# Output weights of an attention kernel: block operations one per slot, second half in the last pair step, left(0) ahead of the last value sums

## The chip, the core and the metric

The kernel runs on one core of one Trainium2 chip. The metric is the device time of one execution in microseconds (us). The core has five engines with instruction streams of their own: PE (matrix products; its weight loads are listed as PEld), DVE, ACT and POOL (elementwise work), and SP, which here issues nearly all DMA transfers, in one order fixed at build time. An engine takes its instructions strictly in order and waits on semaphores for what other engines or transfers have to finish first.

## The reference

Two independent computations on inputs of 2048 rows by 576 columns; their results stand side by side in an output of 2048 x 1152, all float32. Cut to what matters:

```python
# A: attention with a compressive memory, 32 heads of 18 columns, 4 segments of 512 rows
for s in range(4):
    logits = q_s @ k_s.T * 18 ** -0.5 + mask          # mask: -1e9 where the key index is above the query's
    a_dot = softmax(logits) @ v_s
    pq = phi(q_s)                                     # phi(t) = t + 1 if t > 0 else exp(t)
    a_mem = (pq @ M) / (pq @ z + 1e-6)
    o_s = g * a_mem + (1 - g) * a_dot                 # g = sigmoid(beta), one per head
    pk = phi(k_s); M += pk.T @ v_s; z += pk.sum(0)
A = concat(o_s) @ wo                                  # 2048 x 576 by 576 x 576
# B: Fourier mixing, real part of a two-dimensional DFT given as matrices
a = x @ hid_re.T; b = x @ hid_im.T
B = seq_re @ a - seq_im @ b                           # 2048 x 2048 by 2048 x 576, twice
return concat([A, B], axis=-1)
```

The change lies in how the operands of the product `o @ wo` are prepared.

## The kernel before

**Products.** A float32 product is done as three products of rounded parts: an operand is split into a high part (a copy in the rounded type, made on ACT) and a low part (operand minus high part, made on DVE or POOL), and high x low, high x high and low x high are added up in PSUM.

**Stages.** First come the projections and the memory. Then two streams of work are interleaved to the end. `dense()` does the Fourier mixing: `hidden` makes a and b, `sequence` multiplies by the DFT matrices through `product` (PE lines L583 and L628 to L630), whose operand blocks `chi`/`clo` are split as they arrive (L451 on ACT, L456 on POOL), and its result is evacuated into `y` on DVE (L653). `attention()` does the heads. It is a generator over 68 steps p of eight slots each; 64 steps belong to pairs of heads, and the stages of one pair are spread over steps by lags (scores first, softmax parts 2 and 3 steps later, the value products `pv` 4 steps later), so steps 64 to 67 only drain. The main loop runs one slot of `attention()`, then pieces of `dense()` until both streams have used the same share of their estimated time; so an engine's queue holds slots of attention and pieces of dense work in turn. `later(n, ...)` runs a thing n slots later.

**The last steps of attention.** `pv(n)` (L1066, L1067 on PE) multiplies probabilities by values into the one PSUM bank `pv`; `pv_out` (L1079 to L1088 on DVE, "value sums" below) normalises what is there, reads the bank empty and adds the share to `og`. The probabilities' low parts are made by L1049 on DVE. Six slots after the second half of a group of four heads, `turn_out` transposes `og` (L1101, DVE) and its store to `od` follows; after the last group `turn_tails` (L1113) transposes the tails, stores them to `odt`, and one more transfer copies `odt` into `od`.

**The output stage.** `o @ wo` is done by 2 x 2 blocks with seven products instead of eight (p1 to p7), for row tiles n and n + 8 together, n = 0 to 7, in two column halves of `wo`'s inner blocks (c = 0 and 1). It needs combined operands on both sides:

- Right operands, from `wo` in five row blocks `raw[0]` to `raw[4]` (the last is a 64-row tail, held twice). For a half c the blocks are a = c and b = c + 2. `first_block` gives B11, `second_row` B21 and B22, `tails` and `tail_difference` the tail operands. Four subtractions (`difference`, L739) form, in place in `raw`, aR - aL, bR - aR, bR - aL and bL - bR (L and R are the left and right 288 columns); `combined` makes their high parts on ACT (L707) and `combined_low` their low parts on DVE (L710). `block_low` and `row_low` make low parts on POOL (also L710).
- Left operands: `left(n)` (L805 to L846), from the rows that come back from `od`: sums and differences of two row tiles and their splits. For n = 0 its two-operand instructions are on DVE (L825, L828, L829, L832, L833, L837, L840, L843, L845) and its copies on ACT (L826, L830 and others). It is a generator of six pieces.

`o_load` (L687) loads a row tile back from `od`; `o_pair` does that for n and n + 8 into `craw`. In `output_stage`, p7 and p6 and the others issue their products through `seventh` (L848, matmul L857), p7 ends with two `u` sums on DVE (among them L879), and `store` writes rows of the output.

**What sets the order.** All right operands are prepared while attention and the dense work are still running. `right_operands` fills a table `PLAN` at build time: `at(p, slot, fn, ...)` runs `fn` right behind the issue of that slot of step p. So an operation's place in its engine's queue, and that of a DMA in SP's queue, is what the table says. `ready` in the main loop is the generator `left(0)`, which is started at step 67 slot 5 and then takes one piece a slot or piece of dense work.

Of the kernel before, what the change touches and what calls it, by code (L numbers as in the profile page):

```python
# [12 lines left out]
F32 = mybir.dt.float32  # L13
# [9 lines left out]
S, D, H, DH, NSEG, L = 2048, 576, 32, 18, 4, 512  # L23
P = 128
# [16 lines left out]
def infini_attention_and_fnet(ctx: ExitStack, tc: tile.TileContext, xT, wqk, w8, wv, wo, beta, xtT, cT, hT, out):  # L41
    nc = tc.nc
    act, dve, pool, pe = nc.scalar, nc.vector, nc.gpsimd, nc.tensor
# [100 lines left out]
    def wide_tile(cols):  # L144
        return lambda: wide.tile([P, cols], F32R, name="wide", tag="wide")
# [196 lines left out]
    def sums(c):  # L342
        b, at, both = SUMS[c]
        if c < 4:
            return m_ps[b][:, at:at + 1 + both]
        return m_ps[b][:64, at].rearrange("p (k h) e -> p k h e", k=2)
# [349 lines left out]
    def right_operands():  # L696
        raw, late = {}, {}

        def at(p, slot, fn, *a):
            PLAN.setdefault(8 * p + slot, []).append((fn, a))  # L700

        def load(k):
            raw[k] = sb.tile([P, D], F32, name="raw", tag="raw", bufs=3)
            dma(raw[k], wo[k])

        def high(o, k, cs=slice(0, D)):
            act.activation(o, raw[k][:, cs], AF.Copy)  # L707

        def low(engine, o, hi, k, cs=slice(0, D), rows=slice(0, P)):
            engine.tensor_tensor(o[rows], raw[k][rows, cs], hi.bitcast(F32)[rows], OP.subtract)  # L710
# [30 lines left out]
        def stage(i, n):  # L741
            return (sr if i < 2 else sq).tile([P, 4, 256], F32R, name="late", tag=f"{n}s{i}").rearrange("p a x -> p (a x)")

        def combined(c, n):
            k, names = ((c, ("T1", "T3")), (c + 2, ("T4", "T2")))[n]
            if c == 0:
                hi, lo = late["s", n] = [stage(n, x) for x in "qk"]
                lo = [lo[:, L_], lo[:, R_]]
            elif n == 0:
                hi, lo = [stage(2, x) for x in "qk"]  # L750
                lo = [lo[:, L_], lo[:, R_]]
            else:
                hi, lo = wide_tile(D)(), [t[:, D:D + 288] for t in late["s", 0]]
            for i, x in enumerate(names):
                WO[x, c] = hi[:, 288 * i:288 * i + 288], lo[i]
            high(hi[:, :D], k)

        def combined_low(c, n):
            k, names = ((c, ("T1", "T3")), (c + 2, ("T4", "T2")))[n]
            for i, x in enumerate(names):  # L760
                low(dve, WO[x, c][1], WO[x, c][0], k, (L_, R_)[i])

        def block_low(c):
            low(pool, WO["B11", c][1], WO["B11", c][0], c, L_)
# [1 line left out]
        def row_low(c):  # L766
            low(pool, late["r", c][1], late["r", c][0], c + 2)

        at(57, 2, load, 0)
        at(57, 4, load, 2)  # L770
        at(58, 2, first_block, 0)
        at(58, 2, second_row, 0)
        at(58, 2, load, 4)
        at(58, 4, block_low, 0)
        at(59, 4, row_low, 0)
        at(59, 2, tails)
        at(60, 4, lambda: low(pool, late["w"][0], late["w"][0], 4, rows=lower))
        at(61, 4, lambda: low(pool, late["w"][1], late["w"][1], 4, rows=upper))
        at(61, 6, difference, pool, (4, L_), (4, L_), (4, R_))
        at(62, 2, tail_difference)  # L780
        at(62, 4, lambda: low(pool, TAIL[0][0], TAIL[0][0], 4, L_, lower))
        at(62, 6, lambda: low(pool, TAIL[0][1], TAIL[0][1], 4, L_, upper))
        at(62, 6, load, 1)
        at(63, 6, first_block, 1)
        at(64, 4, block_low, 1)
        for c, p in ((0, 64), (1, 66)):
            a, b = c, c + 2
            if c:
                at(65, 6, load, 3)
                at(66, 2, second_row, 1)  # L790
                at(66, 3, row_low, 1)
            at(p, 3 + c, difference, dve, (a, L_), (a, R_), (a, L_))
            at(p, 3 + c, difference, dve, (a, R_), (b, R_), (a, R_))
            at(p, 5 + c, difference, dve, (b, R_), (b, R_), (a, L_))
            at(p, 5 + c, difference, dve, (b, L_), (b, L_), (b, R_))
            for n in range(2):
                at(p + 1, 2, combined, c, n)
                at(p + 1, 3 + n, combined_low, c, n)
        for t in (0, 8):
            at(66, 5, o_load, t, lambda t=t: sq.tile([P, 4, 256], F32, name="oraw", tag="qs3" if t else "ks3").rearrange(  # L800
                "p a x -> p (a x)")[:, :5 * P].rearrange("p (k x) -> p k x", k=5))
        for t, tag in ((1, "phi"), (9, "plo")):
            at(67, 4, o_load, t, lambda tag=tag: sa.tile([P, 5, P], F32, name="oraw", tag=tag, bufs=2))

    def left(n):  # L805
        one, two = O.pop(n), O.pop(n + 8)
# [389 lines left out]
        tick()  # L1196
    td = ta = 0.0
    right_operands()
    ready = None
    for n, w in enumerate(attention()):  # L1200
        tick()
        ta += w
        for fn, a in PLAN.pop(n, ()):
            fn(*a)
        if n == 8 * (NP + V_LAG - 1) + 5:
            ready = left(0)
        if ready:
            next(ready, None)
        while td / total_d < ta / total_a:
            t = next(d, BREAK)  # L1210
            if t is BREAK:
                break
            td += t
    while due:
        tick()
    for t in d:
        tick()
        next(ready, None)
    while due:
        tick()  # L1220
    for _ in ready:
        pass
    output_stage()


# [41 lines left out]
```

## Time and profile before

| | |
|---|---|
| device time, median of 3 runs | 999.08 us (998.12 to 999.17) |
| the profiled execution: time, span, mean granted TensorE clock | 998.66 us, 997.0 us, 0.998 |
| PE busy | 982.3 us, 99% of the span, 9246 instructions |
| PE weight loads busy | 919.6 us, 92% |
| DVE busy | 787.3 us, 79%, 2115 instructions |
| ACT busy | 714.6 us, 72%, 1686 instructions |
| POOL busy | 673.8 us, 68%, 744 instructions |
| DMA | 209.97 MB, mean 211 GB/s |

The time is that of the whole execution on the device; the span is from the first to the last instruction in the trace of one profiled execution. Busy times are sums over that span. A group row names line, engine, operation, result <- operands with their shapes, then count, busy time and the idle time of the engine in front of it with what ended it. In a window row the first number pair is the window in us from the start of the span. Durations in the trace belong to that one execution.

### The profile page before, as it was taken

Reading aid. Unit: us, or ns where it says so; the run is one execution under the profiler, and the core shown is the slowest. Engines: PE = TensorE matmul, PEld = TensorE weight load, DVE = VectorE, ACT = ScalarE, POOL = GpSimd, SP = SyncE. Lnnn points to the kernel's source line nnn. Section 1 sums busy time; section 2 is a strip of 40 time slices with the busy share of each in tenths; the row PEclk is TensorE's granted clock in tenths of the full one; section 3 lists DMA queues with packets and bytes.
Section 4 is the critical chain, followed back from the end, with each engine's and each line's share of the span. In section 5 each row is a group of like instructions: output and inputs, shape, how many; then the busy total and the mean of one; then the engine's idle time right before and its main releaser. Section 6 shows DMA issues by size and latency. Waiting matters only on the chain.

```text
span 997.0 us, 25491 instructions
## 1 busy us (share of the span) xinstructions
PE 982.3 (99%) x9246; PEld 919.6 (92%) x9246; DVE 787.3 (79%) x2115; ACT 714.6 (72%) x1686; POOL 673.8 (68%) x744
## 2 busy tenths in 40 slices
PE   9999999999999999999999999999999999999798
PEld 8989989899999999999999999999999999999798
DVE  6657668594678777888898888788889888989785
ACT  6757576663887877878788888877777777777342
POOL 2657576676767677666766777767766767887371
PEclk9999999999999999999999999999999999999999
DMA  7537456767688899899999987889999999987553
GB/s 240 194 118 252 179 174 242 239 232 228 146 180 214 215 248 226 209 231 230 254 222 251 217 215 200 189 199 215 234 223 230 241 222 247 247 185 184 152 186 114
DMA packets 304351, 209.97 MB, mean 211 GB/s; under 512 B 204992, under 2 KB 259136, under 8 KB 304192
## 3 DMA queue, kind: packets, MB, share of 16 engines
q1 hardware_dynamic: 304000, 208.20, 81.5%
q8 instruction: 72, 1.18, 0.5%
q14 instruction: 55, 0.45, 0.2%
q10 hardware_dynamic: 224, 0.14, 0.0%
HBM read 122.37 MB, written 58.98 MB: 182 GB/s over the span
## 4 chain that ended last, share of the span: by engine, by line
PE 84%; DVE 7%; ACT 4%; issue 2%; POOL 1%; DMA 1%; SPq 0%; POOLq 0%; DVEq 0%; ACTq 0%
PE d L583 37%; PE s L948 7%; PE v L84 4%; PE pv L1066 4%; PE qk L250 4%; PE d L630 3%; PE d L628 3%; PE d L629 3%; PE t L857 2%; PE pv L1067 2%; PE m L363 1%; PE d L857 1%; PE s L857 1%; PE t L1022 1%; PE qk L84 1%
## 5 line engine op out<-in xcount | busy, mean ns | idle before, releaser
L954 DVE CUSTOM_DVE_ANT_0 s<-s,causal 128x128 f32<-128x128 f32 (+3 forms) x512 | 248.5, 503 | 94.7 <-PE s L948 85.6
L456 POOL TENSOR_TENSOR clo<-craw,chi 128x512 fp32r<-128x512 f32 x158 | 218.8, 1385 | 89.0 <-ACT chi L451 60.1
L583 PE MATMUL d<-wide,chi 128*128 128x288 f32 x1408 | 262.5, 303 | 0.7 <-DVE y L653 0.6
L583 PEld LDWEIGHTS d<-wide,chi 128*128 128x128 f32 x1408 | 211.4, 189 | 3.1 <-DVE y L653 1.1
L583 PE MATMUL d<-wide,clo 128*128 128x288 f32 x704 | 173.9, 314 | 0.0
L988 POOL TENSOR_TENSOR hl<-pf,hl 128x768 f16<-128x768 f32 x64 | 113.4, 1772 | 70.4 <-ACT hl L984 56.7
L1034 ACT ACTIVATE phi<-t 128x384 f16<-128x384 f32 x128 | 61.8, 483 | 101.6 <-PE t L1031 101.6
L948 PE MATMUL s<-ks,qs 108*128 108x128 bf16 (+3 forms) x512 | 132.9, 303 | 1.7 <-DVE negm L954 1.2
L977 ACT ACTIVATE pf<-s,nb 128x128 f32<-128x128 f32 (+3 forms) x256 | 128.3, 527 | 6.2
L583 PE MATMUL d<-ab,chi 128*128 128x288 f32 x640 | 123.3, 302 | 0.0
L1049 DVE TENSOR_TENSOR plo<-pf,phi 128x384 f16<-128x384 f32 (+1 forms) x128 | 121.2, 947 | 0.0
L583 PEld LDWEIGHTS d<-wide,clo 128*128 128x128 f32 x704 | 118.3, 189 | 1.4
L1035 ACT ACTIVATE pf<-t 128x384 f32<-128x384 f32 (+1 forms) x192 | 99.5, 518 | 6.4 <-PE t L1022 6.1
L451 ACT ACTIVATE chi<-craw 128x512 fp32r<-128x512 f32 x160 | 100.1, 626 | 0.5 <-DMA craw<-cT 0.3
L583 PEld LDWEIGHTS d<-ab,chi 128*128 128x128 f32 x640 | 97.8, 188 | 0.5
L984 ACT ACTIVATE hl<-pf 128x768 f16<-128x768 f32 (+1 forms) x128 | 87.4, 729 | 2.0
L583 PE MATMUL d<-ab,clo 128*128 128x288 f32 x320 | 83.0, 308 | 0.0
L628 PE MATMUL d<-wide,chi 128*128 128x288 f32 x256 | 81.4, 318 | 0.0
L630 PE MATMUL d<-wide,clo 128*128 128x288 f32 x256 | 75.6, 295 | 0.9 <-POOL clo L456 0.9
L629 PE MATMUL d<-wide,chi 128*128 128x288 f32 x256 | 75.6, 295 | 0.0
L1049 POOL TENSOR_TENSOR plo<-pf,phi 128x384 f16<-128x384 f32 x64 | 61.4, 960 | 12.1 <-ACT pf L1035 11.6
L988 DVE TENSOR_TENSOR hl<-pf,hl 128x512 f16<-128x512 f32 x64 | 68.8, 1075 | 0.1
(281 smaller groups left out, 2526.8 us busy)
## 6 DMA issues: line engine op xcount, KB each, us to landing
craw<-cT SPq DMA_DIRECT2D x128, 256.0 KB
ks<-kd SPq DMA_DIRECT2D x32, 432.0 KB
qs<-qd SPq DMA_DIRECT2D x32, 432.0 KB
craw<-xtT SPq DMA_DIRECT2D x32, 320.0 KB
vd<-vs SPq DMA_DIRECT2D x16, 440.0 KB
vst<-vd SPq DMA_DIRECT2D x32, 220.0 KB
qd<-p SPq DMA_DIRECT2D x16, 384.0 KB
kd<-p SPq DMA_DIRECT2D x16, 384.0 KB
```

Of the source, the lines that this page charges most:

```text
L451: act.activation(hi, raw[:, :4], AF.Copy)
L456: engine.tensor_tensor(lo, raw[:, :4], hi.bitcast(F32), OP.subtract)
L583: pe.matmul(o[h], a, b[:, h * 288:h * 288 + 288], start=start, stop=stop)
L628: pe.matmul(o, xh[:, k], wl[k][:, cs], start=k == 0, stop=False)
L629: pe.matmul(o, xh[:, k], wh[k][:, cs], start=False, stop=False)
L630: pe.matmul(o, xl[:, k], wh[k][:, cs], start=False, stop=False)
L948: pe.matmul(o[:, c:c + w], q[:, i * P:w], k[:, :w], start=True, stop=True)
L954: dve.tensor_tensor_reduce(o[:, c:c + w], o[:, c:c + w], CAUSAL[0][:, L - w:], scale=scale, scalar=-LOWEST, op0=OP.add, op1=OP.min, accum_ ...
L977: act.activation(f[:, FIRST_COL[i]:FIRST_COL[i] + w], o[:, c:c + w], AF.Exp, bias=nb[:, i:i + 1], scale=-1.0)
L988: engine.tensor_tensor(hl[:, 1, a:b], f[:, a:b], hl[:, 0, a:b], OP.subtract)
L1035: act.activation(f[:, r:r + w], o[:, :w], AF.Exp, bias=LIFT, scale=SCALE)
L1049: (pool if kind == 2 else dve).tensor_tensor(lo[:, a:b], f[:, a:b], hi[:, a:b], OP.subtract)
```

## The change

- In the first half (c = 0), the four `difference` subtractions run one to a slot in step 64, slots 3 to 6 (before: two at slot 3, two at slot 5), and the four low parts of `combined_low` one to a slot in step 65, slots 3 to 6 (before: two each at slots 3 and 4).
- In the second half (c = 1), all four subtractions run at step 67, slot 1 (before: step 66, slots 4 and 6), the high parts at step 67, slot 2, as before, and the four low parts at slot 3 (before: slots 3 and 4).
- The high and low parts of that half's second block (T4, T2) lie in spare columns of the tiles of the first half, and the high part is copied in two pieces; no wide tile is taken for it. Block 3 of `wo` is loaded into a wide tile at step 58, slot 4 (before: into a `raw` tile at step 65, slot 6).
- `second_row(1)` moves from step 66, slot 2, to step 61, slot 2, its low part on POOL from step 66, slot 3, to step 62, slot 6. The subtraction of the tails moves from step 61, slot 6, to step 62, slot 4, `tail_difference` from step 62, slot 2, to step 63, slot 2, its two low parts from step 62, slots 4 and 6, to step 63, slots 4 and 6. The load of block 1 moves from step 62, slot 6, to step 63, slot 6, and `first_block(1)` from there to step 64, slot 2.
- `left(0)` is issued whole at step 67, slot 4, behind the loads of row tiles 1 and 9. This is in front of the value sums of the last pair, which are issued at step 67, slot 7. The `ready` handling in the main loop goes.

PE's instructions and their order stay as they are; on the other engines only the operations named here change places.

```diff
--- before.py
+++ after.py
@@ -700,7 +700,7 @@
             PLAN.setdefault(8 * p + slot, []).append((fn, a))
 
         def load(k):
-            raw[k] = sb.tile([P, D], F32, name="raw", tag="raw", bufs=3)
+            raw[k] = wide.tile([P, D], F32, name="wide", tag="wide") if k == 3 else sb.tile([P, D], F32, name="raw", tag="raw", bufs=3)
             dma(raw[k], wo[k])
 
         def high(o, k, cs=slice(0, D)):
@@ -743,64 +743,68 @@
 
         def combined(c, n):
             k, names = ((c, ("T1", "T3")), (c + 2, ("T4", "T2")))[n]
-            if c == 0:
-                hi, lo = late["s", n] = [stage(n, x) for x in "qk"]
-                lo = [lo[:, L_], lo[:, R_]]
-            elif n == 0:
-                hi, lo = [stage(2, x) for x in "qk"]
-                lo = [lo[:, L_], lo[:, R_]]
+            if c and n:
+                hi, lo = ([t[:, D:D + 288] for t in late["s", i]] for i in (1, 0))
             else:
-                hi, lo = wide_tile(D)(), [t[:, D:D + 288] for t in late["s", 0]]
+                late["s", 2 * c + n] = [stage(2 * c + n, x) for x in "qk"]
+                hi, lo = ([t[:, L_], t[:, R_]] for t in late["s", 2 * c + n])
             for i, x in enumerate(names):
-                WO[x, c] = hi[:, 288 * i:288 * i + 288], lo[i]
-            high(hi[:, :D], k)
-
-        def combined_low(c, n):
+                WO[x, c] = hi[i], lo[i]
+            if c and n:
+                for i in range(2):
+                    high(hi[i], k, (L_, R_)[i])
+            else:
+                high(late["s", 2 * c + n][0][:, :D], k)
+
+        def combined_low(c, n, i):
             k, names = ((c, ("T1", "T3")), (c + 2, ("T4", "T2")))[n]
-            for i, x in enumerate(names):
-                low(dve, WO[x, c][1], WO[x, c][0], k, (L_, R_)[i])
+            low(dve, WO[names[i], c][1], WO[names[i], c][0], k, (L_, R_)[i])
 
         def block_low(c):
             low(pool, WO["B11", c][1], WO["B11", c][0], c, L_)
 
         def row_low(c):
             low(pool, late["r", c][1], late["r", c][0], c + 2)
+
+        def sums(c):
+            a, b = c, c + 2
+            return (((a, L_), (a, R_), (a, L_)), ((a, R_), (b, R_), (a, R_)),
+                    ((b, R_), (b, R_), (a, L_)), ((b, L_), (b, L_), (b, R_)))
 
         at(57, 2, load, 0)
         at(57, 4, load, 2)
         at(58, 2, first_block, 0)
         at(58, 2, second_row, 0)
         at(58, 2, load, 4)
+        at(58, 4, load, 3)
         at(58, 4, block_low, 0)
         at(59, 4, row_low, 0)
         at(59, 2, tails)
         at(60, 4, lambda: low(pool, late["w"][0], late["w"][0], 4, rows=lower))
+        at(61, 2, second_row, 1)
         at(61, 4, lambda: low(pool, late["w"][1], late["w"][1], 4, rows=upper))
-        at(61, 6, difference, pool, (4, L_), (4, L_), (4, R_))
-        at(62, 2, tail_difference)
-        at(62, 4, lambda: low(pool, TAIL[0][0], TAIL[0][0], 4, L_, lower))
-        at(62, 6, lambda: low(pool, TAIL[0][1], TAIL[0][1], 4, L_, upper))
-        at(62, 6, load, 1)
-        at(63, 6, first_block, 1)
+        at(62, 4, difference, pool, (4, L_), (4, L_), (4, R_))
+        at(63, 2, tail_difference)
+        at(62, 6, row_low, 1)
+        at(63, 4, lambda: low(pool, TAIL[0][0], TAIL[0][0], 4, L_, lower))
+        at(63, 6, lambda: low(pool, TAIL[0][1], TAIL[0][1], 4, L_, upper))
+        at(63, 6, load, 1)
+        at(64, 2, first_block, 1)
         at(64, 4, block_low, 1)
-        for c, p in ((0, 64), (1, 66)):
-            a, b = c, c + 2
-            if c:
-                at(65, 6, load, 3)
-                at(66, 2, second_row, 1)
-                at(66, 3, row_low, 1)
-            at(p, 3 + c, difference, dve, (a, L_), (a, R_), (a, L_))
-            at(p, 3 + c, difference, dve, (a, R_), (b, R_), (a, R_))
-            at(p, 5 + c, difference, dve, (b, R_), (b, R_), (a, L_))
-            at(p, 5 + c, difference, dve, (b, L_), (b, L_), (b, R_))
-            for n in range(2):
-                at(p + 1, 2, combined, c, n)
-                at(p + 1, 3 + n, combined_low, c, n)
+        for i, x in enumerate(sums(0)):
+            at(64, 3 + i, difference, dve, *x)
+            at(65, 3 + i, combined_low, 0, i // 2, i % 2)
+            at(67, 1, difference, dve, *sums(1)[i])
+            at(67, 3, combined_low, 1, i // 2, i % 2)
+        for n in range(2):
+            at(65, 2, combined, 0, n)
+            at(67, 2, combined, 1, n)
         for t in (0, 8):
             at(66, 5, o_load, t, lambda t=t: sq.tile([P, 4, 256], F32, name="oraw", tag="qs3" if t else "ks3").rearrange(
                 "p a x -> p (a x)")[:, :5 * P].rearrange("p (k x) -> p k x", k=5))
         for t, tag in ((1, "phi"), (9, "plo")):
             at(67, 4, o_load, t, lambda tag=tag: sa.tile([P, 5, P], F32, name="oraw", tag=tag, bufs=2))
+        at(67, 4, lambda: list(left(0)))
 
     def left(n):
         one, two = O.pop(n), O.pop(n + 8)
@@ -1196,16 +1200,11 @@
         tick()
     td = ta = 0.0
     right_operands()
-    ready = None
     for n, w in enumerate(attention()):
         tick()
         ta += w
         for fn, a in PLAN.pop(n, ()):
             fn(*a)
-        if n == 8 * (NP + V_LAG - 1) + 5:
-            ready = left(0)
-        if ready:
-            next(ready, None)
         while td / total_d < ta / total_a:
             t = next(d, BREAK)
             if t is BREAK:
@@ -1215,11 +1214,8 @@
         tick()
     for t in d:
         tick()
-        next(ready, None)
     while due:
         tick()
-    for _ in ready:
-        pass
     output_stage()
 
 
```

## The prediction

> **What bounds the kernel now.** I read the page first, then PE's waits, then the last 85 us window by window, and there the timeline of each engine.
>
> ```profile
> PE 982.3 (99%) x9246; PEld 919.6 (92%) x9246; DVE 787.3 (79%) x2115; ACT 714.6 (72%) x1686; POOL 673.8 (68%) x744
> PE pv L1066 <- ACT l L826: 2.1, 1, 2.1
> PE t L857 <- DVE u L879: 1.9, 1, 1.9
> PE pv L1067 <- DVE plo L1049: 1.6, 2, 1.2
> PE d L583 <- DVE y L653: 0.6, 1, 0.6
> 870.00:880.00 10.00, 10.00 (x112) 9.34 (x111) 8.26 (x28) 7.73 (x20) 9.87 (x11) 1.00 0.82 176
> 920.00:930.00 10.00, 6.66 (x59) 6.34 (x59) 9.83 (x17) 3.12 (x7) 5.30 (x5) 0.90 0.86 224
> 930.00:940.00 10.00, 9.82 (x85) 9.51 (x84) 7.42 (x20) 3.43 (x8) 3.81 (x6) 0.93 0.11 33
> 940.00:950.00 10.00, 8.31 (x61) 8.19 (x62) 7.56 (x16) 3.86 (x9) 3.94 (x6) 1.00 0.63 175
> ```
>
> Columns of the window rows: length, busy us (and instructions) of PE, its weight load, DVE, ACT and POOL, then granted clock, DMA share, GB/s. PE is busy for 99% of the span; its instructions and their order are the same after the change, so time can only come from PE's pauses. The four longest sums are 2.1, 1.9, 1.6 and 0.6 us. They lie near the end: in 920 to 930 PE has 6.66 of 10 us while DVE has 9.83, and the granted clock is down to 0.90 and then 0.93. In that stretch DVE sets the pace, not PE. These are the rows:
>
> ```profile
> 919.14 0.29 PE L583 MATMUL d<-wide,clo 128*128 128x288 f32 x1
> 926.65 0.19 PE L1066 MATMUL pv<-vst,phi 128*128 128x55 bf16 x1 [2.10 <-ACT l L826]
> 928.08 0.21 PE L1067 MATMUL pv<-vst,plo 128*128 128x37 bf16 x1 [1.24 <-DVE plo L1049]
> 941.69 1.06 PE L857 MATMUL t<-late,l 128*128 128x288 f32 x6 [1.87 <-DVE u L879]
> 948.59 1.22 PE t L857 x8
> ...
> 918.55 2.97 DVE L739 TENSOR_TENSOR raw<-raw 128x288 f32<-128x288 f32 x2
> 926.20 0.30 DVE L1088 TENSOR_TENSOR og<-og,pv 128x144 f32<-128x144 f32 x1
> 926.42 1.60 DVE L1049 TENSOR_TENSOR plo<-pf,phi 128x512 f16<-128x512 f32 x1
> 927.94 0.81 DVE L710 TENSOR_TENSOR late<-raw,late 128x288 fp32r<-128x288 f32 x2
> 929.42 0.41 DVE L825 TENSOR_TENSOR ls<-oraw 128x256 f32<-128x256 f32 x1
> 930.09 0.68 DVE L829 TENSOR_TENSOR l<-oraw,l 128x512 fp32r<-128x512 f32 x1
> 933.15 0.22 DVE L1079 RECIPROCAL pv<-pv 128x8 f32<-128x8 f32 x1 [2.38 <-PE pv L1067]
> 934.60 0.30 DVE L1088 TENSOR_TENSOR og<-og,pv 128x144 f32<-128x144 f32 x1
> 934.82 0.42 DVE L832 TENSOR_TENSOR ls<-ls,oraw 128x256 f32<-128x256 f32 x1
> 935.15 0.43 DVE L833 TENSOR_TENSOR lb<-oraw,lb 128x256 fp32r<-128x256 f32 x1
> 935.51 0.49 DVE L1101 STREAM_TRANSPOSE ogt<-og 128x128 f32<-128x128 f32 x2
> 936.12 0.37 DVE L837 TENSOR_TENSOR ls<-oraw,ls 128x256 f32<-128x256 f32 x1
> 936.43 1.23 DVE L840 TENSOR_TENSOR l<-ls,l 128x512 fp32r<-128x512 f32 x1
> 937.69 0.93 DVE L843 TENSOR_TENSOR lb<-oraw,lb 64x128 fp32r<-64x128 f32 x2
> 939.01 0.69 DVE L845 TENSOR_TENSOR l<-ls,l 128x512 fp32r<-128x512 f32 x1
> 939.62 0.45 DVE L653 TENSOR_TENSOR y<-y,d 128x288 f32<-128x288 f32 x1
> 941.19 0.44 DVE L879 TENSOR_TENSOR u<-t,u 128x288 f32<-128x288 f32 x1
> 946.47 0.42 DVE L828 TENSOR_TENSOR ls<-craw 128x256 f32<-128x256 f32 x1 [1.28 <-DMA craw<-od]
> 947.98 0.45 DVE L879 TENSOR_TENSOR u<-t,u 128x288 f32<-128x288 f32 x1
> ```
>
> (Start, length, operation; in brackets the idle time before it and what ended it; the row at 948.59 is a piece of the chain of waits.) PE stops at 924.55, runs one matmul at 926.65 and goes on at 928.08. The first stop is charged to ACT, but in the code the matmul writes the one value-sum bank, which is free only when DVE has read it (L1088, to 926.50). The second stop waits for the low part of L1049, which ends at 928.02 right behind it. Both come from DVE being late, and what makes it late are four weight subtractions (L739) in pair step 66: two took 2.97 us. The third stop, 1.87 us before 941.69, waits for the first `u` sum (L879, ends 941.63), again the end of a DVE queue. The next product of that kind, 6.90 us later at 948.59, starts 0.16 us behind its own `u` sum (947.98 plus 0.45), which sits behind an operand that waited for a DMA (L828): no pause, but no slack either.
>
> ```profile
> 926.50 0.40 ACT L830 ACTIVATE lb<-oraw 128x256 fp32r<-128x256 f32 x1
> 919.56 1.64 POOL L710 TENSOR_TENSOR wide<-raw,wide 128x576 fp32r<-128x576 f32 x1
> 926.20 1.27 POOL L456 TENSOR_TENSOR clo<-craw,chi 128x512 fp32r<-128x512 f32 x1 [2.17 <-DMA od<-ogt]
> ...
> 936.02 0.33 SPq L94 DMA_DIRECT2D od<-ogt  x1
> 938.08 0.70 SPq L94 DMA_DIRECT2D od<-odt  x1
> 940.09 0.34 SPq L94 DMA_DIRECT2D out<-y  x1
> 940.53 3.35 SPq L687 DMA_DIRECT2D craw<-od  x4
> ```
>
> **The change part by part.**
>
> *Second half out of step 66.* The number of operations stays; four L739, in two blocks, leave step 66 and run in step 67 behind the L1049 of 926.42. After the last `y` sum of step 66, possible once PE ends at 919.43, DVE has 919.9. Then come L1049 of the other block (0.5 alone to 1.3 in company, an estimate from the 0.7 to 1.6 of its sister), the value sums (933.15 to 934.90, so 1.75) and L1049 (1.60 before; 0.6 at best): the bank is free at 922.1 to 923.0 and the low part ready at 922.7 to 924.5. PE asks at 924.5. So 3.5 us of stop go, and so does most of the lowered clock behind them. By the windows the clock cost (0.10 + 0.07) x 10 = 1.7 us of full speed, some of it while PE stood anyway; I take 1.5. PE then reaches its third stop not at 939.82 but 10.2 us (939.82 - 928.08 - 1.5) after 924.5: 934.7.
>
> *What stands in step 67 then.* Four L739, four L710, and the whole of left(0). An L710 costs 0.41 (0.81 for two, POOL idle); an L739 contended cost 1.49 (2.97 for two). I take the low price and 0.1 for each of three links: 922.7 + 8 x 0.41 + 0.3 = 926.3. left(0) cannot start before its operand lands, and ACT read that at 926.50. From its rows left(0) costs 0.41 + 0.41 + 0.68 + 0.42 + 0.43 + 0.37 + 1.23 + 0.93 + 0.69 = 5.6 us; starts overlap, so 5.0 to 5.6, and I take 5.3: end 931.8. Then 1.75 for the last value sums: they end at 933.6, where they ended at 934.90. Bounds: 933.2, and 935.8 if the two L456 of POOL left in that stretch each hold up one operation for a full contended surcharge (2 x 1.08).
>
> One row and one rule on that surcharge: two L739 took 2.97 us with POOL at work, two L710 of the same shape 0.81 without. The Trainium skill, page "SBUF — State Buffer", section "SBUF: two separate sides", calls the port pair that VectorE and GpSimd share an exclusive lock, held for a whole instruction. By it each of the two L456 (1.27) could cost DVE at most its own length, 2.5 us in all; the rows give 2.2, and the sum keeps those.
>
> *left(0) in front of the last value sums.* This is the step that can hurt: queued behind left(0) on DVE are the last value sums, their transposes and both last `y` sums; behind those on SP stand the stores to `od`, the copy out of `odt`, the store of `y` and the loads of the next operands. Counted from the end of the value sums: transposes 0.49, then SP from its `od` store to the `odt` copy 2.06 (936.02 to 938.08), that copy 0.70 and 0.05 between, from the `y` store to the operand loads 0.44: 3.74. From their issue to L828 5.94 (940.53 to 946.47), from there to PE at 948.59 2.12. Sum 11.8: PE cannot pass that product before 933.6 + 11.8 = 945.4. Before, the `y` sum, not the `odt` copy, was last ahead of those loads (out at 940.09, sum ended 940.07).
>
> PE itself is there earlier. The third stop: `y` sums two x 0.4 and transposes 0.49 plus about half as much for the tails (an estimate) after 933.6 give 935.1, from the end of the last `y` sum to PE 1.62 (940.07 to 941.69): 936.7. So PE stands 2.0 us there, goes on, comes after 6.9 us to 943.6 and stands again, 1.8 us, a stop that before did not have.
>
> *The rest.* Putting the first half's four subtractions and four low parts one to a slot in steps 64 and 65 alters no count; DVE is full there, and PE's 0.6 us wait for L653 becomes shorter or moves to the next L1049. Zero, bounds -0.6 to +1.1 (one contended surcharge ahead of something PE wants). The second row's low part (L710, 1.64) goes from step 66 to step 62 on POOL, whose window at 870 is 9.87 of 10 full; in exchange one subtraction of tails goes half a step later and two tail parts go to step 63. POOL had pauses there, so zero; if its buffers do not cover it, PE waits up to 1.64. Loading block 3 into a wide tile is one DMA of the same size, earlier; it and the load of block 1 pass SP's queue where each waits on work done by then. ACT's one extra piece falls where it is idle. After 948.59 all that follows hangs on the same loads and moves with them.
>
> **Sum.** 948.59 - 945.4 = 3.2 us. The profiled execution took 998.66 us (span 997.0), 0.42 under the median of 999.08: 998.66 - 3.2 = 995.5. With the ends 933.2 and 935.8 for the value sums, the gain is 3.6 to 1.0.
>
> **The rivals.**
>
> *B, more.* The `odt` copy need not wait for the landing of its source as long as 2.06 us shows, or the loads land sooner. Then PE's own arrival decides: 948.59 - 943.6 = 5.0, so 993.7. For it: the DMA share was 0.11 in 930 to 940, so nothing crowds these transfers. Against it: that was so before, and the 5.94 came out all the same.
>
> *C, less.* Either both L456 collide (gain 1.0, 997.7) or the clock falls again. The trace: after stops of 2.10 and 1.24 the window's clock was 0.90 and 0.93, after the one of 1.87 it was 1.00. The new stops are 2.0 and 1.8, and between them PE runs for 6.9. If the first counts as the long one did, up to 1.5 us comes back, 997.0. The Trainium skill, "TensorE: Matmul & The Clock Gate", section "What's actually happening", says one idle window of about 3.4 us halves the clock; by that rule the new stops are too short, and this half of C falls away. About 997.4.
>
> *D, slower.* left(0) in front makes the last value sums late. The point is 948.59 - 11.8 = 936.8: 3.2 us past my 933.6, three contended surcharges of 1.08. If all eight L739 and L710 cost 1.49, they end at 922.7 + 11.9 = 934.6, the value sums at 934.6 + 5.3 + 1.75 = 941.7, and PE passes at 953.5: 4.9 us slower, 1003.6. For it: in step 66 three of four were contended. Against it: POOL is busy 5.30 and 3.81 of 10 in 920 to 940, and the change takes its 1.64 out.
>
> *E, nothing.* The waits at 926.65 and 928.08 vanish, and their time reappears before 941.69: PE's gain is only in arriving earlier at a queue that ends when it did. That is so if the value sums end at 936 to 937 again: 998 to 999.5.
>
> **How the numbers follow.** Forecast 0.45 with its own range 994.8 to 996.6; B 0.11; C 0.20; E 0.09; D 0.15. A measurement of this kernel tells about 0.2%, 2 us, from no change (the three runs lie 1.05 apart), so faster is below 996.7: forecast, B and a third of C, 0.63. The rest of C and E are within it: 0.22. D is slower: 0.15. The range reaches down to B (993.6) and up through C and the middle of E (998.9); outside are D and the ends, together just below 0.2.
>
> **What would show it.** Right: no PE pause of over 0.5 us at the value products of the last pair; the window's clock 1.00 in 920 to 930; a PE pause of about 2 us before the first product that waits for L883 (formerly L879) and a second one of about 1.8 us at the same product of the next row pair, ended by a `u` sum behind a `craw` load; last value sums ending 1.3 us earlier than before. Wrong: L739 in step 67 at 1.4 us each with POOL beside it (D), a clock below 0.95 after the new pauses (C), no second pause (B), or PE pauses in 870 to 900 that wait for POOL (the moved low part).

## The result and the profile after

The change takes 996.06 us (median of 22 runs, 995.17 to 999.43) against 999.71 us for the kernel before in the same sessions (998.07 to 1002.41). The ratio is 0.997, with a 95% interval of 0.9962 to 0.9978: 0.3% or 3.0 us faster by that ratio; the two medians lie 3.65 us apart. Forecast were 995.5 us and 3.2 us. The profiled execution of the change is a slower one of its kind, 997.69 us with a span of 996.0; why single executions of one kernel differ by 4 us is shown below, and it makes the two spans (997.0 and 996.0) understate the gain.

PE's waits after the change (engine, line, what it waited for, us in total, times, longest):

```profile
PE t L861 <- DVE u L883: 5.0, 2, 3.1
PE pv L1071 <- DVE plo L1053: 0.4, 1, 0.4
```

The three stops of before were 2.1 and 1.2 us at the value products and 1.9 us at the first product that waits for a `u` sum. Now 0.4 us is left at the value products, and the wait for `u` sums is 5.0 us in two stops. The windows (columns as in the prediction) say the same:

```profile
920.00:930.00 10.00, 10.00 (x108) 9.86 (x108) 9.36 (x22) 5.10 (x11) 2.55 (x3) 1.00 0.73 203
930.00:940.00 10.00, 8.10 (x61) 7.86 (x60) 8.21 (x19) 2.79 (x7) 3.92 (x6) 1.00 0.34 98
940.00:950.00 10.00, 6.86 (x40) 6.62 (x39) 5.87 (x11) 3.04 (x8) 5.53 (x7) 0.83 0.56 172
946.00:948.00 2.00, 2.00 (x8) 2.00 (x9) 1.95 (x5) 1.26 (x2) 1.84 (x4) 0.51 0.16 61
948.00:950.00 2.00, 2.00 (x12) 2.00 (x11) 1.93 (x4) 0.04 (x1) 1.84 (x3) 0.64 0.73 247
```

From 920 to 930 PE is busy for 10.00 us (6.66 before) and the clock is 1.00 (0.90 before). The stops stand in 930 to 950, and behind the second one the clock is 0.51 and 0.64. The rows of PE, DVE and SP there:

```profile
935.96 1.07 PE L861 MATMUL t<-late,l 128*128 128x288 f32 x6 [1.90 <-DVE u L883]
946.00 1.80 PE L861 MATMUL t<-late,wide 128*128 128x288 f32 x6 [3.15 <-DVE u L883]
...
921.73 0.45 DVE L739 TENSOR_TENSOR raw<-raw 128x288 f32<-128x288 f32 x1
923.57 0.82 DVE L710 TENSOR_TENSOR late<-raw,late 128x288 fp32r<-128x288 f32 x2
924.31 0.82 DVE L710 TENSOR_TENSOR late<-wide,late 128x288 fp32r<-128x288 f32 x2
925.43 1.26 DVE L829 TENSOR_TENSOR ls<-oraw 128x256 f32<-128x256 f32 x1 [0.31 <-DMA oraw<-od]
929.98 0.69 DVE L849 TENSOR_TENSOR l<-ls,l 128x512 fp32r<-128x512 f32 x1
932.03 0.30 DVE L1092 TENSOR_TENSOR og<-og,pv 128x144 f32<-128x144 f32 x1
935.46 0.45 DVE L883 TENSOR_TENSOR u<-t,u 128x288 f32<-128x288 f32 x1
944.02 0.43 DVE L832 TENSOR_TENSOR ls<-craw 128x256 f32<-128x256 f32 x1 [4.54 <-DMA craw<-od]
...
934.84 0.70 SPq L94 DMA_DIRECT2D od<-odt  x1
935.63 0.38 SPq L94 DMA_DIRECT2D out<-y  x1
936.11 5.31 SPq L687 DMA_DIRECT2D craw<-od  x4
```

DVE runs the four subtractions and four low parts from 921.73 to 925.13, left(0) from 925.43 to 930.67 and the last value sums to 932.33. PE stops 1.90 us before 935.96, and 3.15 us before 946.00 for a `u` sum queued behind an operand that came late from `od` (L832 at 944.02, idle 4.54 us). The trace closes: the second of these products started at 948.59 before and starts at 946.00 now, 2.59 us earlier; the half clock behind it costs 0.49 x 2 + 0.36 x 2 = 1.7 us; 2.59 - 1.7 = 0.9, and the span fell by 1.0.

### The profile page after: what moved, and what is told of

Same layout as the page of the kernel before. It is cut to its first block, busy times and chain, and to the rows that moved or that the text cites. A ratio compares the mean times of both kernels' runs of the same rounds, so it can differ in the third digit from the quotient of the medians.

```text
span 996.0 us, 25495 instructions
## 1 busy us (share of the span) xinstructions
PE 981.4 (99%) x9246; PEld 918.7 (92%) x9246; DVE 783.2 (79%) x2115; ACT 714.0 (72%) x1687; POOL 672.6 (68%) x744
## 4 chain that ended last, share of the span: by engine, by line
PE 82%; DVE 7%; ACT 4%; issue 3%; POOL 2%; DMA 2%; SPq 0%; POOLq 0%; DVEq 0%; ACTq 0%
PE d L583 37%; PE s L952 7%; PE v L84 4%; PE pv L1070 4%; PE qk L250 4%; PE d L630 3%; PE d L628 3%; PE d L629 3%; PE pv L1071 2%; PE t L861 2%; PE m L363 1%; PE t L1026 1%; PE s L861 1%; PE qk L84 1%; PE d L861 1%
## 5 line engine op out<-in xcount | busy, mean ns | idle before, releaser
L456 POOL TENSOR_TENSOR clo<-craw,chi 128x512 fp32r<-128x512 f32 x158 | 217.8, 1379 | 90.7 <-ACT chi L451 67.2
L1053 DVE TENSOR_TENSOR plo<-pf,phi 128x384 f16<-128x384 f32 (+1 forms) x128 | 121.8, 952 | 0.0
L1053 POOL TENSOR_TENSOR plo<-pf,phi 128x384 f16<-128x384 f32 x64 | 61.7, 965 | 12.1 <-ACT pf L1039 8.7
```

The lines of the kernel that those rows point to most:

```text
L456: engine.tensor_tensor(lo, raw[:, :4], hi.bitcast(F32), OP.subtract)
L1053: (pool if kind == 2 else dve).tensor_tensor(lo[:, a:b], f[:, a:b], hi[:, a:b], OP.subtract)
```

## Experiments: which part of the change brings what

Every ratio is against the kernel before, run beside it on the same chip, since its own median moved from 999.65 to 1000.37 us between sessions.

| kernel | median us | ratio to before, 95% interval |
|---|---|---|
| the change | 996.06 | 0.997 (0.9962 to 0.9978) |
| left_spread | 993.74 | 0.9935 (0.9923 to 0.9948) |
| left_front_only | 1001.0 | 1.0009 (0.9997 to 1.0021) |
| second_half_only | 996.47 | 0.9963 (0.995 to 0.9976) |
| second_half_and_slots | 995.53 | 0.9961 (0.9948 to 0.9975) |
| row_late | 997.91 | 0.998 (0.9971 to 0.9989) |
| first_half_in_pairs | 1000.37 | 1.0002 (0.9991 to 1.0013) |
| pairs_tails_back | 997.35 | 0.9982 (0.9972 to 0.9992) |
| loads_early | 993.35 | 0.9935 (0.9922 to 0.9947) |
| before_loads_early | 1000.53 | 1.0004 (0.9991 to 1.0016) |
| u_first_only | 998.34 | 0.9992 (0.9981 to 1.0002) |
| spread_loads | 994.32 | 0.9938 (0.9925 to 0.9951) |
| spread_loads_u_first | 992.68 | 0.9924 (0.9912 to 0.9936) |

**The second half alone.** The edit to the kernel before:

```diff
-            at(p, 3 + c, difference, dve, ...)             # twice
+            at(p + c, 3 - 2 * c, difference, dve, ...)
-            at(p, 5 + c, difference, dve, ...)             # twice
+            at(p + c, 5 - 4 * c, difference, dve, ...)
-                at(p + 1, 3 + n, combined_low, c, n)
+                at(p + 1, 3 + n * (1 - c), combined_low, c, n)
```

> The kernel before the change with one edit: the second half's four subtractions run at step 67 slot 1 and its four low parts at slot 3. left(0), the row's low part on POOL in step 66, the loads and the first half stay as before. Theory: this move alone takes away the two pauses at the value products and so brings most of the gain; the low part on POOL that stays in step 66 costs 1 to 2 us of it (row_late was 1.85 us slower than the change): 994.5 to 996.5 us. Rival 1 (the gain needs the row's low part out of step 66, since POOL then holds up DVE's other work ahead of the value products): 997.5 to 999.5 us. Rival 2 (the pauses only move to the first product that waits for the first u sum): 999 to 1000 us.

It took 996.47 us, as the theory had it, ratio 0.9963: this one move brings as much as the whole change. Its waits of PE (same columns as above):

```profile
PE t L857 <- DVE u L879: 2.1, 1, 2.1
PE t L857 <- DVE l L840: 0.8, 1, 0.8
PE pv L1067 <- DVE plo L1049: 0.4, 1, 0.4
```

The stops at the value products are down to 0.4 us, and the clock is 1.00 from 920 to 930 (it falls later, to 0.64 and 0.50 in the two windows of 2 us from 938, behind the stop of 2.1 us). So the first step of the prediction stands by itself, and the rest of the change adds up to about nothing; it is made of parts that work against each other.

**left(0) in front: a loss.** Two edits, one out of the change and one into the kernel before:

```diff
 left_spread (from the change)
-        at(67, 4, lambda: list(left(0)))
+        (the main loop starts left(0) at step 67, slot 5, one piece per slot or dense piece, as before)
 left_front_only (from the kernel before)
+        at(67, 4, lambda: list(left(0)))
-        (the pieces of left(0) in the main loop)
```

> The changed kernel, but left(0) is issued as before the change: it starts at step 67 slot 5, one piece per slot or piece of dense work, so the last value sums stand behind its first pieces only. Everything else of the change stays. Theory: the gain comes from the four subtractions and their low parts leaving the space ahead of the value products; left(0) in front gives nothing and only delays the last value sums. Then the pauses at the value products stay away, and the last value sums end 1 to 2 us earlier than the 932.33 us of the changed kernel; the time is 994.5 to 996.3 us, equal to the changed kernel's 996.06 or up to 1.5 us better. Rival 1: left(0) in front is what brings the gain (its operands are ready sooner): then most of the gain goes, 998 to 1000 us. Rival 2: both are needed, as the work of left(0) that is left over comes between the value sums and the first u sum: 996.5 to 998 us.

> The kernel before the change with one edit: left(0) is issued whole at step 67 slot 4, in front of the last value sums; the weight operations stay where they were. Theory (left(0) in front is no gain): the pauses of 2.1 and 1.2 us at the value products stay; DVE's idle 2.38 us ahead of the last value sums are filled by left(0), and those end about 936.5 instead of 934.90; with 12 to 13.7 us from there to the second product that waits for a u sum, the time is 999.5 to 1001.5 us, against 999.7 for the kernel before. Rival 1 (left(0) in front brings the gain): 996 to 997 us.

left_spread took 993.74 us: without this part the change is twice as good. left_front_only took 1001.0 us, no gain and perhaps a small loss. The times are as the theory had it, left_spread 0.8 us beyond its range on the good side. The value sums moved otherwise than it said: in left_spread they end 3.2 us earlier (1 to 2 forecast), and in left_front_only they end at 934.71, not at 936.5, with a second stop of PE of 3.13 us behind them. The rows of left_spread:

```profile
935.94 1.07 PE L861 MATMUL t<-late,l 128*128 128x288 f32 x6 [2.01 <-DVE u L883]
942.99 1.06 PE L861 MATMUL t<-late,wide 128*128 128x288 f32 x6 [0.15 <-DVE u L883]
...
928.86 0.30 DVE L1092 TENSOR_TENSOR og<-og,pv 128x144 f32<-128x144 f32 x1
940.99 0.43 DVE L832 TENSOR_TENSOR ls<-craw 128x256 f32<-128x256 f32 x1 [1.54 <-DMA craw<-od]
...
932.34 0.70 SPq L94 DMA_DIRECT2D od<-odt  x1
934.35 0.34 SPq L94 DMA_DIRECT2D out<-y  x1
934.78 3.61 SPq L687 DMA_DIRECT2D craw<-od  x4
```

The first stop is as long as in the change (2.01 against 1.90 us). But the last value sums end at 929.16 instead of 932.33, the copy out of `odt` is issued at 932.34 instead of 934.84, and the operand of the second pair is read at 940.99 instead of 944.02: the second stop is 0.15 instead of 3.15 us. In this execution the clock also stayed at 1.00 behind the first stop. That is not the whole difference: at an equal mean clock of 0.999 three runs of left_spread have a median of 993.16 us and six of the change one of 995.71.

**The row's low part on POOL.** The edit to the change:

```diff
-        at(61, 2, second_row, 1)
-        at(62, 6, row_low, 1)
+        at(66, 2, second_row, 1), at(66, 3, row_low, 1)
```

> The changed kernel, but the second row's high parts and its low part on POOL (L710, 1.64 us before the change) run in step 66 slots 2 and 3 as before the change, not in steps 61 and 62. Theory: this move counts for little; POOL's low part now lengthens one or two DVE operations of step 66 by up to 1.1 us each, of which PE sees at most 1: 996 to 997 us. Rival: the move out of step 66 is what freed DVE there (the four subtractions were slow because POOL worked on the row beside them), so most of the gain goes: 998 to 1000 us.

It took 997.91 us, 1.85 us more than the change by the medians and 1.0 by the ratios, between theory and rival.

```profile
919.51 1.74 POOL L710 TENSOR_TENSOR wide<-wide 128x576 fp32r<-128x576 f32 x1
922.24 1.74 POOL L456 TENSOR_TENSOR clo<-craw,chi 128x512 fp32r<-128x512 f32 x1
...
922.75 1.54 DVE L739 TENSOR_TENSOR raw<-raw 128x288 f32<-128x288 f32 x1
924.33 0.46 DVE L739 TENSOR_TENSOR raw<-wide,raw 128x288 f32<-128x288 f32 x1
...
937.98 1.38 PE L861 MATMUL t<-late,l 128*128 128x288 f32 x6 [3.01 <-DVE u L883]
```

The same L456 in the change:

```profile
919.97 1.28 POOL L456 TENSOR_TENSOR clo<-craw,chi 128x512 fp32r<-128x512 f32 x1
```

The low part itself (1.74 us at 919.51) touches no subtraction. It pushes POOL's next L456 from 919.97 to 922.24, and that one runs beside the first subtraction: 1.54 us against 0.46 for the next. The first stop of PE becomes 3.01 us, 1.1 more than in the change. By the Trainium skill, page "SBUF — State Buffer", section "SBUF: two separate sides", the port pair of VectorE and GpSimd is an exclusive lock held for a whole instruction; the surcharge of 1.08 us, below the 1.74 us of the L456 beside it, agrees with that.

**The first half, one per slot or in pairs.** The prediction put this at zero.

```diff
-            at(64, 3 + i, difference, dve, *x)
-            at(65, 3 + i, combined_low, 0, i // 2, i % 2)
+            at(64, 3 + i // 2 * 2, difference, dve, *x)
+            at(65, 3 + i // 2, combined_low, 0, i // 2, i % 2)
```

> The changed kernel, but the first half's subtractions and low parts stand in pairs as before (step 64 slots 3 and 5, step 65 slots 3 and 4), not one to a slot. Theory: it makes no difference, since DVE is full there in either order and PE's pauses there are 0.6 us at most: 995.5 to 996.7 us. Rival (the smaller pieces keep DVE's answers to PE short and are part of the gain): 997 to 998.5 us, with a PE pause of about 1 us between 890 and 915.

1000.37 us: the whole gain is gone, more than even the rival said. The rows, first of this kernel, then of the kernel before at the same place:

```profile
902.58 0.53 PE L583 MATMUL d<-wide,chi 128*128 128x288 f32 x2 [1.91 <-DVE y L653]
...
889.92 1.57 DVE L1053 TENSOR_TENSOR plo<-pf,phi 128x384 f16<-128x384 f32 x1
896.06 2.35 DVE L739 TENSOR_TENSOR raw<-raw 128x288 f32<-128x288 f32 x2
900.27 1.89 DVE L739 TENSOR_TENSOR raw<-raw 128x288 f32<-128x288 f32 x2
...
889.39 0.80 POOL L710 TENSOR_TENSOR wide<-raw,wide 64x288 fp32r<-64x288 f32 x1
891.15 1.01 POOL L710 TENSOR_TENSOR wide<-raw,wide 64x288 fp32r<-64x288 f32 x1
```

```profile
901.55 0.53 PE L583 MATMUL d<-wide,chi 128*128 128x288 f32 x2 [0.64 <-DVE y L653]
...
890.16 0.56 DVE L1049 TENSOR_TENSOR plo<-pf,phi 128x384 f16<-128x384 f32 x1
895.03 2.33 DVE L739 TENSOR_TENSOR raw<-raw 128x288 f32<-128x288 f32 x2
899.21 1.92 DVE L739 TENSOR_TENSOR raw<-raw 128x288 f32<-128x288 f32 x2
```

PE waits 1.91 us for the `y` sum behind the second pair, where it waited 0.64 before. The pairs themselves are not longer (2.35 and 1.89 us against 2.33 and 1.92); they come 1.03 us later, 0.8 of it because L1053 ahead of them took 1.57 us instead of 0.56. Beside it POOL now makes the two low parts of the tails (889.39 and 891.15), which the change moved into step 63. A test of that:

```diff
 first_half_in_pairs, and
-        at(62, 4, difference, pool, ...); at(63, 2, tail_difference); ... low parts at (63, 4), (63, 6)
+        at(61, 6, difference, pool, ...); at(62, 2, tail_difference); ... low parts at (62, 4), (62, 6)
```

> first_half_in_pairs (1000.37 us) with the tails' four POOL operations back in steps 61 and 62; the row's low part stays in step 62, slot 6. Theory: the pause of 1.91 us there came from the two tail parts that the change put into step 63, where POOL lengthened DVE's L1053 (1.56 instead of 0.56 us) ahead of the paired subtractions; with the tails back, the pause is 0.6 to 0.9 us again and the time 996 to 998 us. Rival (the row's low part in step 62, or the pairs themselves beside the other loads, make the pause): it stays above 1.5 us, 999 to 1001 us.

997.35 us, and the wait is shorter again:

```profile
PE d L583 <- DVE y L653: 0.8, 1, 0.8
```

So the move of the tails costs the pairs a longer stop. The way there is not only the one that the theory named: L1053 still took 1.15 us in this run, the first pair began 0.85 us earlier (895.21), and the second pair took 0.97 us instead of 1.89, since POOL's L456 beside it was nearly over (898.62 to 899.91; 900.08 to 901.36 in first_half_in_pairs). One subtraction per slot repays the stop: in the change L1053 took 1.56 us too, but only three of the four subtractions, 2.49 us instead of 4.24, stand ahead of that `y` sum, and the same wait is below 0.2 us. On its own, one per slot is worth little:

```diff
 second_half_only, and the first half's operations at (64, 3 + i) and (65, 3 + i)
```

> second_half_only (996.47 us) with one more edit: the first half's subtractions and low parts one to a slot, as in the change; the row's low part on POOL, the tails and left(0) stay as before. Theory: this takes the pause of 0.6 us in front of the product that waits for L653 (902 us) and nothing else, 995.7 to 996.4 us; what then still lies between it and left_spread (993.74) is the row's low part in step 66. Rival (one per slot is worth 2 us or more by itself): 993 to 994.7 us.

995.53 us, 0.2 below the theory's range, ratio 0.9961 against 0.9963 for second_half_only: the wait for L653 is gone from PE's list, and the difference lies inside the intervals. The rival is out. What is left between this and left_spread (0.9935) is made up of the moves of the row and the tails, the moved loads and the changed tiles; none of them was added to this kernel alone.

## Experiments: the second stop

**The loads of the next operands.** `od` rows of tiles 2, 10, 3 and 11 were stored long before; only SP's order puts their loads behind the last stores.

```diff
-        at(67, 4, lambda: list(left(0)))
+        at(67, 4, lambda: [list(left(0)), o_pair(2), o_pair(3)])
-            if n < 6:
+            if 2 <= n < 6:
                 o_pair(n + 2)
```

> The changed kernel with one edit: the four loads of row tiles 2, 10, 3 and 11 into craw are issued at step 67 slot 4, right behind left(0), so that on SP they stand ahead of the last stores to od and odt, of the copy out of odt and of the store of y, which they do not need. Theory: the second pause of PE (3.15 us in the profile of the change, before the second row pair's product that waits for L883) comes only from these loads standing behind those transfers, and the clock of 0.57 behind it from the pause: both go, 991.5 to 993.5 us. Rival 1: the pause is bound by the arithmetic of left(2) on DVE, ACT and POOL and only becomes shorter, 994 to 995.3 us. Rival 2: the loads are slow wherever they stand, or delay the stores and so the later loads: 996 us or more.

> The kernel before the change with one edit: the four craw loads at step 67 slot 4, as in loads_early. Theory: the second pause exists only because the change lets PE arrive earlier; before it, PE reaches that product when its u sum is ready, so the time stays within 0.2%: 999 to 1001 us. Rival (these loads were worth 2 us or more before the change too): 996 to 998 us.

loads_early took 993.35 us, at the slow end of the theory's range; PE has one stop left, 1.87 us before 937.24. The same edit in the kernel before gave 1000.53 us, ratio 1.0004: there was nothing to win, because PE did not come to that product any earlier. The second stop is made by the change.

**The two remedies together.** spread_loads is left_spread with the same loads at step 67, slot 4.

> left_spread with the four craw loads issued at step 67 slot 4, as in loads_early. Theory: the two edits take away the same second pause, of which left_spread has 0.15 us left; so they don't add up: 993.0 to 994.0 us, as each alone. Rival (they act on different things and add up): 990.5 to 991.5 us.

994.32 us, 0.3 above the theory's range; the ratio is 0.9938 against 0.9935 for each alone. Both take away the same stop, and nothing adds up.

**The first stop.** For the first row pair the evacuation goes ahead of left(1)'s piece:

```diff
                 next(piece)
-                next(prepare, None)
-                next(piece, None)
+                n and next(prepare, None)
+                next(piece, None), n or next(prepare, None)
```

> The changed kernel with the u sum L883 put ahead of left(1)'s pieces, as in spread_loads_u_first, but with the loads and left(0) as in the change. Theory: the first pause falls from 1.9 to about 0.8 us and the second, bound by the craw loads on SP, grows by the same 1.1: no change of the time beyond 0.5 us, 995.5 to 996.6 us. Rival (each pause counts by itself): 994.5 to 995.2 us.

> spread_loads with one more edit: for the first row pair each piece of left(1) is issued behind the evacuation of the product beside it, not in front, so that the u sum L883 stands ahead of left(1)'s L832 and L833 on DVE. Theory: the pause that is left, 2.0 us in front of the first product that waits for L883, is DVE's queue; it becomes 0.8 to 1.0 us, and the chance that the clock halves behind it falls too: 991.3 to 992.8 us. Rival 1 (the wait is for left(0)'s last low part, or left(1) is then late): 993 to 994 us.

In the change alone this made things worse: 998.34 us, where the theory said 995.5 to 996.6. The stop in PE's timeline, then the clock in the windows (columns as above):

```profile
946.32 1.81 PE L861 MATMUL t<-late,wide 128*128 128x288 f32 x6 [4.63 <-DVE u L883]
```

```profile
944.00:946.00 2.00, 0.00 (x0) 0.00 (x0) 1.67 (x3) 0.91 (x4) 1.52 (x2) 0.86 0.25 63
946.00:948.00 2.00, 1.68 (x7) 1.69 (x8) 1.95 (x5) 1.25 (x2) 1.84 (x3) 0.50 0.00 0
948.00:950.00 2.00, 2.00 (x10) 2.00 (x10) 1.97 (x5) 0.02 (x1) 1.92 (x3) 0.50 0.81 288
950.00:952.00 2.00, 2.00 (x10) 2.00 (x9) 0.75 (x2) 0.93 (x2) 1.53 (x2) 0.50 0.90 261
952.00:954.00 2.00, 2.00 (x16) 2.00 (x16) 1.02 (x3) 2.00 (x6) 0.94 (x2) 0.93 0.30 78
```

The first stop is gone, and PE stands 4.63 us in one piece instead of 1.90 + 3.15: as the theory had it, PE only arrives earlier at loads that come when they did (946.32 against 946.00). What the theory lacked in this execution is the clock. By these windows it is half for (0.14 + 0.50 + 0.50 + 0.50 + 0.07) x 2 / 0.5 = 6.8 us, in the change for (0.49 + 0.36) x 2 / 0.5 = 3.4. From 946.32 on, while PE works, that costs 0.50 x 1.68 + 0.50 x 2 + 0.50 x 2 + 0.07 x 2 = 3.0 us of full speed, against 1.7. The other runs point the same way: of the 11, seven have a mean clock of 0.996, three 0.997 and one 0.998, while 16 of the change's 22 have 0.998 or 0.999.

With left(0) spread and the loads early, the same edit pays: spread_loads_u_first took 992.68 us, ratio 0.9924 (0.9912 to 0.9936), the best kernel here and 0.46% below the change. Its stops are 0.8 and 0.5 us, and no window of 2 us from 880 to 960 is below a clock of 1.00.

## Why the prediction was right, and where it was wrong

- *Second half out of step 66:* right. second_half_only shows it alone. The stops of 3.5 us went. The lowered clock behind them did not go but moved: it cost 1.7 us from 926 to 932 before, and costs 1.7 us behind the new second stop in the profiled execution.
- *The queue of step 67:* eight operations in 3.40 us (3.58 forecast with its links), left(0) in 5.24 (5.3), value sums in 1.74 (1.75). The start was forecast 1.0 us too late, 922.7 instead of 921.73, by two terms. The last `y` sum of step 66 does not need PE's end at 919.43: it ran at 917.59, ahead of the PE products that end at 918.71, and DVE was free at 919.06 and then waited 0.21 us for PE. And PE's value products there came 0.73 us earlier (918.55 instead of 919.28), mostly because its wait for L653 in step 64 was gone too; the prediction had kept the clock times of before. So the value sums ended at 932.33, not 933.6.
- *From the value sums to PE, 11.8 us:* measured 13.67. Up to the issue of the loads 3.78 us (3.74 forecast), behind L832 1.98 (2.12). The term that was mis-sized is the one between: loads to L832, 7.91 us instead of 5.94. In the change the loads' issue follows the end of the `odt` copy's by 0.57 us and takes 5.31 us; before, it followed by 1.75 us and took 3.35. left_front_only, row_late and u_first_only have 0.58 us and 5.28, 5.14, 5.32; left_spread has 1.74 and 3.61. Counted from the issue of the `odt` copy, L832 (L828 before) comes after 9.18 us in the change and in left_front_only, after 8.39 before and 8.65 in left_spread: the loads, issued 1.2 us sooner behind that copy, did not land sooner. A time that was measured behind a pause was added behind none. That bytes of the copy and of `y` are still in the queues is the likely reason, and is only argued.
- *Both errors nearly cancel:* 932.33 + 13.67 = 946.00, where 945.4 was forecast. The two stops were 1.90 and 3.15 us (2.0 and 1.8 forecast). So it is partly luck that 995.5 lies so near 996.06: PE passed that product 2.59 us earlier, not 3.2, and the clock behind the second stop, which the sum left to rival C, took another 1.7 us in the profiled execution.
- *left(0) in front:* the prediction saw that this could hurt, priced the chain behind it and then counted the sum as a gain. It never asked what the change would be without it. left_spread shows that it takes back about as much as the change gives.
- *"The rest", zero:* near as a sum only. With pairs, the tails' move costs 2 us by the ratios and 3 by the medians (first_half_in_pairs against pairs_tails_back); one per slot repays it; the row's move brings 1 to 1.9. The bounds were -0.6 to +1.1. With pairs PE's wait rose by 1.3, and behind it the clock fell:

```profile
904.00:906.00 2.00, 2.00 (x12) 1.86 (x12) 1.90 (x5) 1.96 (x5) 1.38 (x1) 0.50 0.84 287
```

- *Rival C:* its sign, a clock below 0.95 behind the new stops, is there in the profiled execution (0.83 from 940 to 950), and it happens in a part of the executions. Of the change's 22 runs, 6 with a mean clock of 0.999 have a median of 995.71 us and 4 with 0.996 have 999.01. Of the two L456 that C and the bounds feared, one met DVE, at L829 of left(0) (1.26 us). *E* did not come, but its mechanism, arriving earlier at a queue that ends when it did, is what u_first_only shows at the second stop. *B* and *D* did not come: all eight weight operations ran at 0.41 to 0.46 us each.

## What to carry to other kernels

When a change gives one engine its operands earlier, follow the same chain to the next thing in a fixed order that cannot come earlier; here four loads that depended on nothing recent stood behind stores that did. Judge a bundle of moves by taking each out again: one move here brought all the gain, another cost as much as that, and two more largely cancelled each other. A stop of PE can cost more than its length: here one of 4.63 us cost more than two of 1.90 and 3.15.

## What the runs showed of the hardware

The granted clock fell to half for about 3.4 us after some stops, and for 6.8 us after two, one of 4.63 us in u_first_only and one of 3.04 us in first_half_in_pairs. What a stop does is not fixed by its length: behind 1.87 us in loads_early the clock fell,

```profile
937.24 1.08 PE L861 MATMUL t<-late,l 128*128 128x288 f32 x6 [1.87 <-DVE u L883]
```

```profile
938.00:940.00 2.00, 2.00 (x13) 2.00 (x12) 1.34 (x3) 0.00 (x0) 1.84 (x3) 0.71 0.28 103
940.00:942.00 2.00, 2.00 (x10) 2.00 (x10) 2.00 (x4) 1.24 (x4) 0.76 (x1) 0.50 0.18 76
942.00:944.00 2.00, 2.00 (x16) 2.00 (x16) 1.37 (x4) 1.84 (x6) 1.18 (x3) 0.94 0.03 10
```

a loss of (0.29 + 0.50 + 0.06) x 2 = 1.7 us, while behind 2.01 us in left_spread (the rows above) every window from 936 to 954 is at 1.00. The same stop shows both: at the first product that waits for a `u` sum, PE stands 1.87 us in the kernel before, with a clock of 1.00 from 940 to 950; in before_loads_early it stands 1.87 us there too, and the clock falls:

```profile
941.98 1.75 PE L857 MATMUL t<-late,l 128*128 128x288 f32 x6 [1.87 <-DVE u L879]
```

```profile
942.00:944.00 2.00, 2.00 (x8) 2.00 (x9) 0.43 (x1) 0.00 (x0) 1.67 (x3) 0.52 0.13 45
```

The price is seen in loads_early: the profiled execution, with the fall, took 995.60 us, the other four took 993.06 to 993.45. In the prediction a rule of the Trainium skill ("TensorE: Matmul & The Clock Gate", section "What's actually happening": half clock after one idle window of about 3.4 us) was read as making stops of 2 us harmless. The runs say otherwise: stops shorter than that window can halve the clock. The same section says that the window runs freely; that a stop counts by how it falls in a window would fit both cases, and is argued, not shown. The 4 us over which one kernel's runs spread go with it in the main, as the medians by clock under rival C show. Over 67 runs in the sessions of the experiments the mean clock of the kernel before is 0.9965, over the change's 22 runs it is 0.9978; by an estimate from these two means, 0.0013 of 996 us, about 1.3 of its 3.0 us are clock.
